# One masking instruction instead of two on GpSimd, routing's units spread over the attention stages, and a new order at the experts' entry

## The chip, the cores and the metric

The kernel runs on one core of a Trainium2 chip. The metric is the device time of one execution in microseconds (us); less is better. Engines are named as in the profile: PE (TensorE matmuls), PEld (TensorE weight loads), DVE (VectorE), ACT (ScalarE), POOL (GpSimd) and SP (SyncE, which issues most transfers).

## The reference

Attention with 4 sink keys and a causal window of 128 runs on 4 batches of 8 heads, 768 positions and a head dimension of 64. Its output, 3072 tokens of 512 numbers, goes through a mixture of experts: 4 groups of 4 experts, the best group and in it the best expert for each token, a hidden layer of 1024.

```python
scores = np.where(is_sink | in_window, scale * q @ k.T, -1e9)
a = np.exp(scores - scores.max(-1)); a = a / (a.sum(-1) + 1e-9)
x = (a @ v)                       # as [3072, 512]
g_idx = argmax(x @ w_group); g_w = softmax(x @ w_group)[g_idx]
e_idx = argmax(x @ w_expert[g_idx]); e_w = softmax(...)[e_idx]
out[token] = g_w * e_w * (relu(x @ w1[g, e]) @ w2[g, e])
```

## The kernel before

**Attention.** The first part is a loop over `i` from 0 to 25 (`NI` is 24). Each pass, called stage i here, works on three tiles of 128 tokens at once: the scores and exponentials of tile i, the transposes and the products with the values of tile a = i-1, and the normalisation of tile b = i-2. Stages with i below 24 are "live"; stages 24 and 25 only finish tiles. All engine queues run in program order, so the order of the calls in the loop is the order in each queue.

Each tile has two halves g of four heads. `scores` writes `ps` on PE. `maxima(i, g, between)` on DVE first runs a predicated copy on `ps` and then four fused subtract-and-reduce instructions (`sm`, CUSTOM in the trace); it calls `between` after the copy, after the second and after the fourth of these, so a stage has six places between maxima. `exps` runs on ACT. `trans` transposes on PE, `evac` copies to `pw` on ACT, and `halves(i, g)` on POOL multiplies the four diagonal blocks of `pw` once by each of two triangle masks `tri`: one product goes to blocks 8 to 11, the other stays in blocks 0 to 3. `values` is the product of `pw` with the values on PE. It needs both products. For the second half it runs in the next stage, behind that stage's first scores. `out_evac` (ACT), `natural` and `logits` (PE) follow; `norm` (DVE) writes `xt`, which SP stores to DRAM (`xd`). `norm_logits` (DVE) writes `lw`, and `add_heads` (POOL) sums it one stage later. The logits lie in the same PSUM tile as the scores of the first half.

**Routing.** When a batch of 6 tiles has its logits, a generator (`route_batch`) turns them into expert choices and positions. Each `yield` ends one unit of one to three small instructions. A label that it yields says where the next unit may run: `"pe"` only where the loop calls `routing(1, ("pe",))`, `"rd"` only where `("rd",)` is named, None anywhere. A stage has a quota (`UNITS`, or `REND`): units run singly in the six places between maxima and behind the second half's transposes (`unit(4)`, before `norm`), and what is left of the quota runs at the end of the stage in one go. Near the end a batch builds two one-hot arrays, `bf` and `af`, in two parts of three tiles each, and PE multiplies them into the table `tab`. Batch 0 starts in stage 8, batch 1 in stage 14, batch 2 in stage 20, batch 3 behind stage 25. Batch 1 also picks the first expert (`pick_id`, which makes `id0` known), batch 2 the second.

**Weights.** Weights come in chunks of 128 by 1024 numbers through `rw`. Each is split into a high part (`whi`, ACT) and the remainder (`wlo`, DVE), in live stages in two halves, one per stage. From stage 15 on, `prefetch` loads one chunk in odd stages and in stages 21 to 23, if the expert is known. A chunk's first half is split two stages after its load or later, when the loop's own clock says that it has landed.

**Entry.** In stages 24 and 25 the first expert's work (`ew`) is mixed in by `next(ew)`: two transposes of gathered tokens, then groups of layer 1 (12 matmuls each, which need the first four chunks). The last 128 rows of that expert are gathered by POOL when batch 2 has been added to `tab`, and PE transposes them behind the seventh group. After stage 25 the rest of the experts runs, bound by PE.

Of the kernel before, what the change touches and what calls it, by code (L numbers as in the profile page):

```python
# [16 lines left out]
ALU = mybir.AluOpType  # L17
# [5 lines left out]
P = 128  # L23
B, H, S, D = 4, 8, 768, 64
NT = S // P
NI = B * NT
# [5 lines left out]
NE = G * EG  # L32
# [22 lines left out]
DVELAG = 1.5  # L55
XLEAD = 9
PEGAP = 1.6
REND, TSTEP = 6, 16
UNITS = {7:4,8:7,9:6,10:6,11:6,12:6,13:6,14:6,15:6,16:6,17:6,18:6,19:6,20:6,21:6,22:6,23:6}
HC = 3  # L60
LATE = 6
PELAG = 2.0
# [72 lines left out]
def moe_attention(tc, kqT, vN, vS, nsw, wgx, w1, w2, out):  # L135
    nc = Pinned(tc)
    v = nc.vector
    with ExitStack() as top, ExitStack() as att:
# [15 lines left out]
        def const(shape, dt, name):  # L154
            return cp.tile(shape, dt, name=name)
# [97 lines left out]
        dq = gp.tile([P, D], F32, name="xg")  # L253
# [35 lines left out]
        tri = const([P, 2, D], F32, "tri")  # L289

        def other_masks():
            v.tensor_scalar(tri[:, 0], dq, 0.0, None, ALU.is_le)
            v.tensor_scalar(tri[:, 1], dq, 0.0, None, ALU.is_gt)
            v.tensor_copy(m4[:, 2, ::BW // NSK], m4[:, 0, ::BW // NSK])
            v.tensor_copy(msk[:, 1], msk[:, 2])
            v.tensor_tensor(snk[0:D], snk[0:D], isu[0:D], ALU.mult)
            v.tensor_tensor(mc[0:D, 1], mc[0:D, 1], snk[0:D], ALU.add)
# [58 lines left out]
        def route_batch(i0, nb, lt, wk, pt, tab, na, pick=None):  # L356
            def sm(shape, name, dt=F32):
                return wk.tile([P, MAXB] + shape, dt, name=name, bufs=1)[:, 0:nb]

            on = nc.gpsimd if pt is None and not tail else v  # L360
# [26 lines left out]
            oh = wk.tile([P, nb, NE], BF16, name=f"oh{nb}", bufs=1)  # L387
# [16 lines left out]
            pe = sm([NE], "pe")  # L404
# [42 lines left out]
            af = wk.tile([P, MAXB, NE, na], F32R, name=f"af{na}", bufs=1)  # L447
            bf = wk.tile([P, MAXB, P], F32R, name="bf", bufs=1)
            for j0 in range(0, nb, 3):
                j1 = min(nb, j0 + 3)  # L450
                w = j1 - j0
                v.tensor_tensor(bf[:, j0:j1], colm[:, None, :].to_broadcast([P, w, P]),
                                ga[:, j0:j1, None].to_broadcast([P, w, P]), ALU.is_equal)
                yield 2
                v.tensor_tensor(af[:, j0:j1], oh[:, j0:j1, :, None].to_broadcast([P, w, NE, na]),
                                av[:, j0:j1, None, :].to_broadcast([P, w, NE, na]), ALU.mult)
                if j1 < nb:
                    yield 2
            yield "pe"
            tt = misc(pt)[:, 0:NE * na]  # L460
            for j in range(nb):
# [204 lines left out]
        state = dict(issued=0, done=0, freed=0, credit=0.0, route=0.0, clk=0.0, at=0.0, dma=0.0, gap=PELAG, dve=0.0)  # L666
# [71 lines left out]
        def lg(i):  # L738
            o = 3 * BW + NSK
            if i < NI - 2:  # L740
                return psb[0][:, :, o:o + 2 * PW]
            if "lg" not in env[i]:
                env[i]["lg"] = spare()[:, 0:NDC * 2 * PW].rearrange("p (c n) -> p c n", c=NDC)
            return env[i]["lg"]
# [67 lines left out]
        def halves(i, g):  # L812
            pw = env[i]["pw", g]
            if i % NT:
                for k in (1, 0):
                    nc.gpsimd.tensor_tensor(pw[:, 8 * k:8 * k + 4], pw[:, 0:4],
                                            tri[:, k, None, :].to_broadcast([P, 4, D]), ALU.mult)

        def sink_copy(i):
            src = env[i]["pt"].rearrange("p m b l x -> p m (b l x)")[:, :, SW - NSK:SW + NSK]  # L820
# [27 lines left out]
        def values(i, g):  # L848
            pw = env[i]["pw", g]
            new, old = vts[i], vts.get(i - 1) if i % NT else None  # L850
            quarters(g, 0, P, new[:, 0], lambda d, j: pw[d, 2 * j:6 + 2 * j:5], start=g == 0)
            quarters(g, D, D, new[:, 1], lambda d, j: pw[d, 1 + 2 * j], stop=g == 1 and old is None)
            if old is not None:
                quarters(g, 0, P, old[:, 1], lambda d, j: pw[d, 4 + 2 * j:10 + 2 * j:5])
                quarters(g, 0, D, old[:, 0], lambda d, j: pw[d, 8 + 2 * j], stop=g == 1)
# [11 lines left out]
        def logits(i):  # L867
            for c in range(NDC):
                for f in range(2):
                    q = slice(f * D, (f + 1) * D)  # L870
                    nc.tensor.matmul(lg(i)[q, c], env[i]["xT"][:, c, q], wsd[:, c], start=True, stop=True)
# [39 lines left out]
                pick = {SNAP: 0, SNAPB: 1, len(BATCHES) - 1: 2}.get(k)  # L911
                rb.append([[(id(lt), x) for x in range(nb)], route(bounds[k], nb, lt, pick), None])

        def routing(k, kinds=(None, "pe", "rd")):
            while k > 0:
                if not rb or not have.issuperset(rb[0][0]):
                    return False
                kind = rb[0][2] if isinstance(rb[0][2], str) else None
                if kind not in kinds or (kind == "pe" and state["clk"] < state["at"]):
                    return False  # L920
                rb[0][2] = r = next(rb[0][1], "end")
                k -= r if isinstance(r, int) else 1
                if tail:
                    dve(0.6 if kind == "rd" else 0.25)
                state["at"] = max(state["clk"] + state["gap"], state["dve"] + 0.4)
                if rb[0][2] == "end":
                    rb.pop(0)
            return True
# [272 lines left out]
        quota = [0]  # L1201

        def unit(k):
            if quota[0] > 0 and routing(1, (None,)):
                quota[0] -= 1

        ew = early_work(PARTS[0][0])
        load_s(0)
        for i in range(NI + 2):
            live = i < NI  # L1210
            quota[0] = UNITS.get(i, REND)
            a, b = i - 1, i - 2
            mid, old = 0 <= a < NI, 0 <= b < NI
# [23 lines left out]
            if mid:  # L1237
                sink_copy(a)
                halves(a, 0)
            if not live:  # L1240
                next(ew)
                if not mid:
                    state["at"] = 0.0
                    routing(1, ("pe",))
            if mid:
                if not live:
                    next(ew)
                sink_t(a)
                trans(a, 1)
# [23 lines left out]
            if old:  # L1273
                natural(b)
            state["clk"] += 3.0
            if live and mid:
                values(a, 0)
            if old:
                logits(b)
            if i % 2 == 0 and 0 < i <= NI:  # L1280
                sums(i - 1)
            if not live:
# [13 lines left out]
            if live:  # L1296
                if mid:
                    halves(a, 1)
                exps(i, 1)
                trans(i, 0)  # L1300
                routing(1, ("rd",))
                unit(4)
                if old:
                    norm(b)
                if later and not gates:
                    gather(*later.pop(0))
                if late:
                    late()
                put_gates(2)
                routing(quota[0], (None, "rd"))  # L1310
            else:
                if mid:
                    next(ew)
                    values(a, 1)
                put_gates(MAXB)
                routing(TSTEP, (None, "rd"))
            if old:
                del env[b]
            if i >= CHOOK and (i % 2 or i > NI - 4):
# [299 lines left out]
```

## Time and profile before

| | us |
|---|---|
| median of three runs (lowest, highest) | 498.94 (498.5, 501.04) |
| profiled execution | 499.12 |
| its span, first to last instruction | 497.3 |
| PE, DVE, ACT, POOL busy in the span | 466.5, 347.0, 326.1, 170.3 |

The span leaves out 1.8 us around the program. Busy times are sums over the whole span; the attention part (about the first 157 us) and the expert part have different limits, so they are read apart.

### The profile page before, as it was taken

What the parts mean: (1) busy time and instruction counts of PE and PEld (TensorE: products, weight loads), DVE (VectorE), ACT (ScalarE), POOL (GpSimd) and SP (SyncE); (2) the same over time, 40 slices, a digit from 0 to 9 for tenths busy, and PEclk for the clock granted to TensorE, in tenths of its full rate; (3) what the DMA queues carried; (4) which work ended last, traced back from release to release, by engine and by line L of the source; (5) the groups of instructions that cost most, each with busy time, mean ns of one, the idle gap of its engine ahead of it and who ended that gap; (6) DMA issues with size and microseconds to landing.
All of it is one profiled execution on the core that took longest, in us unless ns stands there. A gap on an engine that the chain in (4) does not pass through costs nothing.

```text
span 497.3 us, 15548 instructions
## 1 busy us (share of the span) xinstructions
PE 466.5 (94%) x5865; PEld 396.2 (80%) x5865; DVE 347.0 (70%) x1147; ACT 326.1 (66%) x875; POOL 170.3 (34%) x303
## 2 busy tenths in 40 slices
PE   7999889988788998999999999999999999999995
PEld 6788778767667877889897967897879788877894
DVE  6677877897895777796137334844688888787870
ACT  4899779788774332575147247663878877687861
POOL 3565674583766002414020205120503071204021
PEclk9999999999998998999999999999999999999999
DMA  6566557476765529689215277986978997858200
GB/s 192 174 204 217 166 171 214 155 223 213 222 191 162 180 85 355 230 240 373 91 48 150 60 253 239 370 292 229 327 293 298 408 388 273 315 186 332 66 25 30
DMA packets 49556, 107.47 MB, mean 216 GB/s; under 512 B 8932, under 2 KB 9444, under 8 KB 49472
## 3 DMA queue, kind: packets, MB, share of 16 engines
q1 hardware_dynamic: 45008, 93.17, 56.0%
q0 software_dynamic: 4320, 12.94, 7.3%
q8 instruction: 48, 0.79, 0.7%
q10 hardware_dynamic: 144, 0.28, 0.2%
q14 instruction: 36, 0.29, 0.2%
HBM read 93.58 MB, written 12.93 MB: 214 GB/s over the span
## 4 chain that ended last, share of the span: by engine, by line
PE 65%; DVE 11%; ACT 9%; issue 8%; POOL 4%; DMA 2%; POOLq 0%; SPq 0%; DVEq 0%; ACTq 0%
PE po L105 29%; PE ph L105 29%; ACT pt L105 5%; PE tp L105 4%; PE ps L105 3%; POOL pw L105 2%; DVE wlo L105 2%; ACT pw L105 2%; DVE sm L105 1%; DVE xt L105 1%; ACT whi L105 1%; DMA qb<-in_kqT 1%; DVE ps L105 1%; POOL out L105 1%; DVE req L105 1%
## 5 line engine op out<-in xcount | busy, mean ns | idle before, releaser
L105 DVE TENSOR_TENSOR wlo<-rw,whi 128x1024 fp32r<-128x1024 f32 (+1 forms) x116 | 135.8, 1196 | 29.0 <-ACT whi L105 28.4
L105 PE MATMUL ph<-un,whi 128*128 128x256 f32 (+9 forms) x576 | 128.6, 313 | 0.0
L105 PE MATMUL po<-whi,un 128*128 128x512 f32 (+6 forms) x384 | 127.4, 397 | 0.0
L105 POOL DMA_INDIRECT out<-ot,sidx x33 | 41.0, 1244 | 225.4 <-ACT ot L105 169.6
L105 ACT CAST whi<-rw 128x1024 fp32r<-128x1024 f32 (+1 forms) x116 | 114.7, 1018 | 3.4 <-PE po L105 2.3
L105 PE MATMUL ph<-un,wlo 128*128 128x160 f32 (+10 forms) x416 | 99.5, 264 | 0.9 <-DVE wlo L105 0.9
L105 PEld LDWEIGHTS ph<-un,whi 128*128 128x128 f32 x576 | 93.8, 189 | 2.3 <-issue 1.0
L105 PEld LDWEIGHTS po<-whi,un 128*128 128x128 f32 (+5 forms) x384 | 70.6, 185 | 19.7 <-issue 2.1
L105 ACT ACTIVATE pt<-sm,st 128x136 f32<-128x136 f32 x192 | 76.3, 404 | 11.6 <-DVE st L105 11.4
L105 PE MATMUL po<-wlo,un 128*128 128x512 f32 (+7 forms) x200 | 78.7, 393 | 2.2 <-DVE wlo L105 2.2
L105 PEld LDWEIGHTS ph<-un,wlo 128*128 128x128 f32 x416 | 76.8, 189 | 1.5 <-DVE wlo L105 1.1
L105 POOL TENSOR_TENSOR pw<-pw,tri 128x256 f32<-128x256 f32 x80 | 60.1, 752 | 16.2 <-ACT pw L105 12.7
L105 DVE CUSTOM_DVE_ANT_0 sm<-ps,msk 128x136 f32<-128x136 f32 x192 | 46.9, 294 | 6.2 <-PE ps L105 1.1
L105 PE MATMUL po<-pw,vv 64*64 64x128 f32 (+1 forms) x1408 | 40.9, 252 | 9.9 <-POOL pw L105 6.2
L105 PEld LDWEIGHTS po<-pw,vv 64*64 64x64 f32 x1408 | 35.1, 135 | 17.8 <-POOL pw L105 8.5
L105 POOL DMA_INDIRECT xg<-xd,gidx x33 | 35.6, 1077 | 33.6 <-DVE idz L105 16.1
L105 PEld LDWEIGHTS po<-wlo,un 128*128 128x128 f32 (+6 forms) x200 | 36.0, 180 | 10.6 <-DVE wlo L105 2.6
L105 PE MATMUL ps<-kb,qb 64*64 64x204 f32 (+1 forms) x768 | 41.4, 330 | 2.7 <-DVE lw L105 2.2
L105 DVE TENSOR_TENSOR hc<-ph,hc 128x160 f32<-128x160 f32 (+6 forms) x64 | 21.4, 336 | 27.6 <-ACT hc L105 27.6
L105 ACT ACTIVATE un<-ph 128x256 fp32r<-128x256 f32 (+1 forms) x40 | 15.4, 384 | 35.7 <-PE ph L105 35.2
L105 ACT ACTIVATE ot<-po,cg 128x512 f32<-128x512 f32 (+7 forms) x25 | 17.0, 681 | 31.8 <-PE po L105 31.7
L105 ACT ACTIVATION_READ_ACCUMULATOR pt<-sm,st 128x1 f32 x192 | 37.2, 194 | 0.0
(200 smaller groups left out, 659.5 us busy)
## 6 DMA issues: line engine op xcount, KB each, us to landing
rw<-in_w SPq DMA_DIRECT2D x128, 512.0 KB, 5.5
kb<-in_kqT SPq DMA_DIRECT2D x23, 272.0 KB, 4.1
qb<-in_kqT SPq DMA_DIRECT2D x24, 256.0 KB, 3.5
vv<-in_vN SPq DMA_DIRECT2D x24, 256.0 KB, 3.5
xd<-xt SPq DMA_DIRECT2D x24, 256.0 KB, 2.4
xg<-xd,gidx POOLq DMA_INDIRECT x33, 5.9
out<-ot,sidx POOLq DMA_INDIRECT x33, 5.8
sv<-in_vS SPq DMA_DIRECT2D x4, 128.0 KB, 4.9
```

The lines of the kernel that those rows point to most:

```text
L105: r = f(*a, **k)
```

## The change

Six edits. `halves` issues one POOL instruction over both triangles, with the order of the masks in `tri` turned round. The quota is 8 in every stage, and the remainder no longer runs in one go: one unit more, `unit(5)`, runs at the end of the stage. `bf` and `af` get a label of their own, `"hv"`, one part for each live stage, at its end, and `af` goes to the engine called `on`, which is POOL for batches that start in a live stage. In live stages `logits(b)` comes ahead of `values(a, 0)`. In stage 25 the first `next(ew)` is gone. In stage 24 `values(a, 1)` comes ahead of a `next(ew)` instead of behind it.

```diff
-REND, TSTEP = 6, 16
-UNITS = {7:4,8:7,9:6,10:6,11:6,12:6,13:6,14:6,15:6,16:6,17:6,18:6,19:6,20:6,21:6,22:6,23:6}
+REND, TSTEP = 8, 16
+UNITS = {}
...
-            v.tensor_scalar(tri[:, 0], dq, 0.0, None, ALU.is_le)
-            v.tensor_scalar(tri[:, 1], dq, 0.0, None, ALU.is_gt)
+            v.tensor_scalar(tri[:, 1], dq, 0.0, None, ALU.is_le)
+            v.tensor_scalar(tri[:, 0], dq, 0.0, None, ALU.is_gt)
...
+                yield "hv"
                 v.tensor_tensor(bf[:, j0:j1], colm[:, None, :].to_broadcast([P, w, P]),
                                 ga[:, j0:j1, None].to_broadcast([P, w, P]), ALU.is_equal)
-                yield 2
-                v.tensor_tensor(af[:, j0:j1], oh[:, j0:j1, :, None].to_broadcast([P, w, NE, na]),
+                on.tensor_tensor(af[:, j0:j1], oh[:, j0:j1, :, None].to_broadcast([P, w, NE, na]),
                                 av[:, j0:j1, None, :].to_broadcast([P, w, NE, na]), ALU.mult)
-                if j1 < nb:
-                    yield 2
...
-                for k in (1, 0):
-                    nc.gpsimd.tensor_tensor(pw[:, 8 * k:8 * k + 4], pw[:, 0:4],
-                                            tri[:, k, None, :].to_broadcast([P, 4, D]), ALU.mult)
+                nc.gpsimd.tensor_tensor(pw.rearrange("p (k b) q -> p k b q", k=3)[:, ::-2],
+                                        pw[:, None, 0:4].to_broadcast([P, 2, 4, D]),
+                                        tri[:, :, None, :].to_broadcast([P, 2, 4, D]), ALU.mult)
...
-        def routing(k, kinds=(None, "pe", "rd")):
+        def routing(k, kinds=(None, "pe", "rd", "hv")):
...
-            if not live:
-                next(ew)
-                if not mid:
-                    state["at"] = 0.0
-                    routing(1, ("pe",))
+            if i == NI + 1:
+                state["at"] = 0.0
+                routing(1, ("pe",))
             if mid:
                 if not live:
+                    next(ew)
                     next(ew)
...
+            if old:
+                logits(b)
             if live and mid:
                 values(a, 0)
-            if old:
-                logits(b)
...
-                routing(quota[0], (None, "rd"))
+                unit(5)
+                routing(1, ("hv",))
             else:
                 if mid:
+                    values(a, 1)
                     next(ew)
-                    values(a, 1)
                 put_gates(MAXB)
-                routing(TSTEP, (None, "rd"))
+                routing(TSTEP, (None, "rd", "hv"))
```

## Rows read from the trace of the kernel before

**Rows 1.** Stretch; busy PE, PEld, DVE, ACT, POOL; PE's clock; DMA share, GB/s.

```profile
120.00:140.00 20.00, 16.18 (x420) 13.36 (x420) 17.04 (x76) 14.74 (x59) 12.20 (x21) 1.00 0.72 218
...
152.00:153.00 1.00, 1.00 (x18) 0.88 (x12) 0.00 (x0) 0.33 (x1) 0.92 (x2) 0.50 0.28 47
```

**Rows 2.** Timeline of SP's queue: start and length of stores of `xt`.

```profile
21.16 0.34 SPq L105 DMA_DIRECT2D xd<-xt  x1
...
47.34 0.34 SPq L105 DMA_DIRECT2D xd<-xt  x1
...
150.54 0.33 SPq L105 DMA_DIRECT2D xd<-xt  x1
```

**Rows 3.** Timeline of DVE: first unit of a stage's remainder, next predicated copy.

```profile
60.02 0.16 DVE L105 TENSOR_TENSOR runb<-runb,rs 128x16 bf16<-128x16 bf16 x1
...
60.93 0.42 DVE L105 COPY_PREDICATED ps<-selu,ps 128x256 f32<-128x256 int32 x1
...
128.53 0.28 DVE L105 TENSOR_TENSOR rdt<-lt,row 128x120 f32<-128x120 f32 x1
...
130.94 0.41 DVE L105 COPY_PREDICATED ps<-selu,ps 128x256 f32<-128x256 int32 x1
```

**Rows 4.** Timeline of DVE: maxima of stage 16 (six units) and 19 (none).

```profile
97.62 0.42 DVE L105 COPY_PREDICATED ps<-selu,ps 128x256 f32<-128x256 int32 x1
...
100.95 0.18 DVE L105 TENSOR_REDUCE rc<-sacc 128x16 f32<-128x32 f32 x1
...
117.28 0.42 DVE L105 COPY_PREDICATED ps<-selu,ps 128x256 f32<-128x256 int32 x1
...
120.24 0.32 DVE L105 TENSOR_TENSOR lw<-ps,rc 128x160 f32<-128x160 f32 x1
```

**Rows 5.** Instructions grouped by shape: count, busy us, mean ns, idle before.

```profile
L105 POOL TENSOR_TENSOR pw<-pw,tri 128x256 f32<-128x256 f32 x80 | 60.1, 752 | 16.2 <-ACT pw L105 12.7 <-DVE st L105 0.3
L105 POOL TENSOR_TENSOR lt<-lw 128x20 f32<-128x20 f32 x23 | 5.6, 242 | 1.8
L105 DVE TENSOR_TENSOR bf<-colm,row 128x384 fp32r<-128x384 f32 x6 | 3.6, 603 | 0.0
L105 DVE TENSOR_TENSOR af<-oh,av 128x336 fp32r<-128x336 bf16 x6 | 3.3, 550 | 0.0
L105 DVE SCALAR_TENSOR_TENSOR req<-rdt,row 128x120 f32<-128x120 f32 x4 | 2.7, 679 | 0.1
```

**Rows 6.** Timeline: the same `req` instruction with POOL busy and without.

```profile
128.84 1.04 DVE L105 SCALAR_TENSOR_TENSOR req<-rdt,row 128x120 f32<-128x120 f32 x1
129.01 1.53 POOL L105 TENSOR_TENSOR pw<-pw,tri 128x256 f32<-128x256 f32 x2
...
168.88 0.28 DVE L105 SCALAR_TENSOR_TENSOR req<-rdt,row 128x120 f32<-128x120 f32 x1
```

**Rows 7.** Waits up to 180 us: engine, releaser; total us, times, longest.

```profile
PE po L105 <- POOL pw L105: 6.2, 11, 2.1
...
DVE lw L105 <- POOL pw L105: 3.8, 6, 1.2
```

**Rows 8.** Timeline around the end of stage 23, all engines.

```profile
147.54 0.35 POOL L105 TENSOR_TENSOR cw<-rss 128x96 f32<-128x96 f32 x1 [1.11 <-DVE rss L105]
...
151.12 1.50 PE L105 MATMUL po<-pw,vv 64*64 64x128 f32 x32 [2.15 <-POOL pw L105]
```

**Rows 9.** Timeline of the first layer-1 group and the weight splits beside it.

```profile
157.23 0.28 PE L105 MATMUL ph<-un,wlo 128*128 128x256 f32 x1
157.24 0.71 DVE L105 TENSOR_TENSOR wlo<-rw,whi 128x512 fp32r<-128x512 f32 x1
...
161.99 1.23 DVE L105 TENSOR_TENSOR wlo<-rw,whi 128x1024 fp32r<-128x1024 f32 x1 [2.62 <-ACT whi L105]
```

**Rows 10.** Timeline: PE transposes the first expert's last gathered rows.

```profile
171.83 0.63 PE L105 MATMUL ph<-ident,xg 128*128 128x128 f32 x4 [1.23 <-DMA xg<-xd,gidx]
```

**Rows 11.** The chain that ended last: one layer-1 group of the first expert.

```profile
158.99 1.62 PE ph L105 x12
```

## Prediction
> **What bounds the kernel now.** I read the busy times by stretch first. Over the whole span PE is the busiest engine, and behind the entry it hardly waits. In the attention part that turns round: in 120 to 140 us DVE is busy for 17.0 of 20 us, PE for 16.2 [rows 1]. The reader is to see that no engine is full there; each waits for another in turn.
>
> The stores of `xt` give the pace. There is one each stage: from 21.16 to 47.34 us, before any routing, five stages take 26.2 us, 5.24 each. The next sixteen take 103.2 us up to 150.54 [rows 2]. At the old pace they would take 83.8, so 19.4 us are lost in stages 8 to 23, where routing and the first weight splits join in.
>
> Then DVE's own timeline. The remainder of a quota runs behind `norm` in one go, so the next predicated copy, and with it the maxima, starts later by all of it: 0.91 us in stage 9, 2.41 in stage 20 [rows 3]. A unit between maxima costs far less: with six of them stage 16 takes 3.33 us from its first copy to the end of its maxima, stage 19 without any 2.96 [rows 4], 0.06 each. The copy and the maxima leave gaps into which a small instruction fits.
>
> The table of waits shows the other coupling: PE waits for POOL's masked `pw` 11 times, 6.2 us in all, and DVE's `lw` 6 times, 3.8 us [rows 7]. The second is indirect: `lw` needs the logits, which stand in PE's queue behind the `values` that wait for `pw`.
>
> **The change part by part, against the profiled execution's 499.12 us.**
>
> *Routing's units.* Before, six stages (8, 9, 14, 15, 20, 21) run five units each in one go. I take the mean of the two shown, 1.66 us: 10.0 us. 24 small units lie between maxima, 1.5 us. Five pairs of `bf` and `af` lie there too, at 0.60 and 0.55 us [rows 5] 5.8 us. The sum, 17.3, accounts for most of the 19.4. After, I count 42 units between maxima by walking through the generator: 2.5 us. Ten stages get a `unit(5)` behind `norm`; at 0.30 each (a fifth of 1.66 is 0.33) 3.0 us. Five `bf` at stage ends are 3.0. `af` moves to POOL; by POOL's line below it takes 0.9 us there, behind `halves(a, 1)` and ahead of the next stage's first mask. DVE so sheds 17.3 - 8.5 = 8.8 us, from which the next item is taken.
>
> *The longer POOL instruction.* The `req` of stage 20 starts at 128.84 us and ends when POOL's first mask, begun at 129.01, is over: 1.04 us, against 0.28 with POOL quiet [rows 6]. The mean of the four is 0.68 [rows 5], so each loses 0.40 on average. POOL's line through 20 elements at 242 ns and 256 at 752 [rows 5] gives 512 elements 1.30 us, in place of 1.50 for two. The bounds are 1.30 (one fixed part saved) and 1.50 (none). A wait of 0.40 behind 0.75 grows to 0.69 behind 1.30. Of about 27 small units with two operands in SBUF I let one in three be hit: 9 by 0.29 is 2.6 us, between nothing (waits fall rarer, as POOL is held for less) and 7.8. The relief left is 6.2 us. A stage cannot go under 5.24, PE's pace, so I let two thirds reach the end: **-4.1**, with bounds 0 and -6.2.
>
> The Trainium skill, page "SBUF — State Buffer", section "Who interferes with whom", says that a DVE instruction with two SBUF inputs and a GpSimd one that reads SBUF exclude each other for the whole of an instruction. The pair shown agrees [rows 6]. By that rule alone merging lengthens every hold; the rows cannot say how many are hit, so it is a rival below.
>
> *The earlier end of the mask.* A pair takes 1.53 [rows 6], one instruction 1.30, so PE's 11 waits could shrink by 0.2 each, 2.5 at most. Most lie in stages that DVE paces: **-0.5**.
>
> *Logits ahead of `values(a, 0)`.* This takes `lw` out from behind `pw`: 3.8 us at most, but several of the six stages are paced by PE: **-0.8**. What could go wrong is that `logits` wait for the first half's maxima (same PSUM tile) with `values` now queued behind them; 0 is the other bound.
>
> *`cw` later on POOL.* `rss` becomes the last unit between maxima in stages 17 and 23 instead of the fourth. POOL's `cw` waits for it (1.11 us before [rows 8]), and behind `cw` on POOL are `add_heads` and `halves(a, 1)`, for which PE's next `values` wait: 2.15 us at 151.12 [rows 8]. About 2 us of instructions that stood behind `rss` now precede it, less `bf` and `af` (1.15), so PE waits some 1 us longer in stage 24. **+1.0**, between 0 and 2 (stage 18 as well).
>
> *Weights come two stages later.* This is not written in the diff. `id0` was known at the end of stage 15, in time for that stage's `prefetch`. Now stage 15 gets through only two of `pick_id`'s units, the rest follow in stage 16, and the next `prefetch` is in stage 17. One chunk fewer is split by stage 24: six `wlo` halves in place of eight. In stages 17 to 23 that takes two halves off DVE, **-1.2** (bounds 0 and -1.9). In stage 24 the fourth chunk must be split whole before the first layer-1 group can end. PE needed its low part at 157.23; DVE's half split ends at 157.95, and a whole one of 1.23 behind it at 159.18 [rows 9]: **+1.9**. On SP the next loads are then issued within that group, ahead of the loads that the end of the stage issued before.
>
> *Entry order.* In stage 25 `natural`, `logits`, `norm` and the table's last matmuls move ahead of one layer-1 group of 1.62 us [rows 11], and so do the store of `xt` on SP, the gather on POOL and batch 3's units. PE's wait of 1.23 us for that gather [rows 10] is shorter than the group: **-1.2**, or 0 if the earlier stall eats the lead. In stage 24 `values(a, 1)` and a group change places; both are issued anyway: 0. The group hides the evacuation of `xT` on ACT; without that cover it would be under 1 us.
>
> The sum: -4.1 - 0.5 - 0.8 + 1.0 - 1.2 + 1.9 - 1.2 = **-4.9**: 499.1 becomes 494.2. The median of the runs is 0.2 lower than the profiled execution, well inside the runs' own spread, so I give 494.2 for both.
>
> **The rivals.** *The lock takes it back* (no change). If every small two-operand unit meets a POOL mask (27 by 0.29 is 7.8 us), relief falls to 1.0 us, two thirds of it 0.7, and the sum to -1.5: 497.6. For it: `req` is hit in the mean of four. Against: POOL is held for less time in all.
>
> *The entry decides* (slower). The late first chunk costs 1.9 us, and `cw` up to 2.0. A PE that has stood still runs at half clock afterwards: the granted clock is 0.50 at 152 to 153 us, 1.2 instead of 2.4 GHz, after the wait of 2.15 [rows 1, 8]; that `values` block took 1.50 us. A second such stretch of 2 to 3 us at half speed costs 1 to 1.5. With the gather's gain lost this is +1.9 + 2.0 + 1.5, 5.4 us; it decides once the attention part gives back under 3 us, and with 2 us given back the time is 502.5. For it: all of it stands on PE's path. Against: the attention stages have 19.4 us of slack to give.
>
> *The spreading does not speed stages* (no change). If PE is the real limit in the routing stages, one third of the relief arrives, -2.1, and the sum is -2.9: 496.2, on the edge. Against: PE is idle for a fifth of 120 to 140 us [rows 1].
>
> **How the numbers follow.** The time forecast is 494.2, chance 0.50 with its neighbours from 491 to 496.4. The lock has 0.16, the spreading that brings little 0.14, the entry 0.20. About 0.5%, 2.5 us, is what a measurement tells from no change. Faster by more holds the forecast and a good third of the third rival: 0.55. Within it: 0.25. Slower: 0.20. The range starts from the sum with full relief (-6.2) and both POOL terms at their far ends (-2.5, -3.8 together in place of -1.3), 487 at the very least; these do not fall together, so I cut at 490. Above it takes in the lock and most of the entry case, 501.5. The forecast's own range is 491 to 496.4.
>
> **What would show it.** Right: 40 masks of 128x512 near 1.30 us; predicated copies closer behind `xt` in stages 9, 10, 15, 21 and 22; a pace under 6 us for stages 8 to 23 (6.45 before); `wlo` halves x6; no wait of PE for the last gather. Wrong: DVE units of over 1.2 us beside a mask (the lock); PE's wait in stage 24 well over 3 us, or a new stretch at half clock (the entry). If the masks take 1.5 us or more, the POOL terms fall. If stages 13 and 19, which now hold the wait for the table's matmuls, grow by over 1 us each, spreading has only moved the loss.

## The result and the profile after

The changed kernel takes 492.77 us (median of four runs, 491.73 to 493.08); the kernel before, beside it, 499.0 (498.5 to 501.04). The ratio is 0.9864 with a 95% interval of 0.9833 to 0.9895, so the change is faster by some 6.8 us of 500. The profiled execution took 493.08 us with a span of 490.8, against 499.12 and 497.3: 6.0 us less where the sum forecast 4.9. The number is close. What follows shows that its parts are not. (The spans differ by 6.5 us: 2.3 us of the execution now lie outside the span instead of 1.8. Every kernel below with the routing edits has 2.1 to 2.3 us there, every other 1.7 to 1.9; why was not looked into.)

Instructions grouped by shape up to 175 us (count, busy us, mean ns, idle before), to be held against [rows 5]:

```profile
L105 POOL TENSOR_TENSOR pw<-pw,tri 128x512 f32<-128x512 f32 x40 | 52.2, 1304 | 12.7 <-ACT pw L105 12.0 <-DVE st L105 0.3
...
L105 DVE TENSOR_TENSOR wlo<-rw,whi 128x512 fp32r<-128x512 f32 x6 | 5.2, 864 | 0.0
L105 POOL TENSOR_TENSOR af<-oh,av 128x336 fp32r<-128x336 bf16 x6 | 4.7, 786 | 0.0
...
L105 DVE SCALAR_TENSOR_TENSOR row<-ga,row 128x6 f32<-128x6 f32 x3 | 3.0, 991 | 0.0
...
L105 DVE SCALAR_TENSOR_TENSOR req<-rdt,row 128x120 f32<-128x120 f32 x4 | 1.1, 278 | 0.0
```

The merged mask takes the 1.30 us that the line through two sizes gave; `wlo` halves are six; `req` is at its quiet length of 0.28 instead of 0.68. Another unit has taken its place beside the masks: `row`, which the same view of the kernel before has at 0.16 us, takes 0.99 on average. On DVE's timeline one of the three lasts 1.26 us, over the 1.2 that I had named as a sign of the lock; POOL's mask runs beside it from 142.45 to 143.73.

```profile
L105 DVE SCALAR_TENSOR_TENSOR row<-ga,row 128x6 f32<-128x6 f32 x3 | 0.5, 160 | 0.0
```

```profile
142.49 1.26 DVE L105 SCALAR_TENSOR_TENSOR row<-ga,row 128x6 f32<-128x6 f32 x1
```

Stores of `xt` in the timeline of SP's queue, to be held against [rows 2]:

```profile
20.91 0.34 SPq L105 DMA_DIRECT2D xd<-xt  x1
...
48.46 0.34 SPq L105 DMA_DIRECT2D xd<-xt  x1
...
148.42 0.36 SPq L105 DMA_DIRECT2D xd<-xt  x1
```

From 48.46 to 148.42 there are sixteen stages of 6.25 us each, where they took 6.45 before and I had named under 6 as a sign of being right. Here is the first surprise: attention has hardly become faster. The maxima did move up, as DVE's timeline shows (stage 9, and stage 20, where the same `req` stands as in [rows 6]):

```profile
59.95 0.16 DVE L105 TENSOR_TENSOR runb<-runb,rs 128x16 bf16<-128x16 bf16 x1
60.03 0.41 DVE L105 COPY_PREDICATED ps<-selu,ps 128x256 f32<-128x256 int32 x1
...
127.53 0.28 DVE L105 TENSOR_TENSOR rdt<-lt,row 128x120 f32<-128x120 f32 x1
127.73 0.42 DVE L105 COPY_PREDICATED ps<-selu,ps 128x256 f32<-128x256 int32 x1
128.06 0.28 DVE L105 SCALAR_TENSOR_TENSOR req<-rdt,row 128x120 f32<-128x120 f32 x1
```

The copy follows 0.08 and 0.20 us behind the unit, where it came 0.91 and 2.41 later [rows 3]. But new waits stand elsewhere. The table of waits up to 175 us (total us, times, longest), against [rows 7]:

```profile
POOL cw L105 <- DVE rss L105: 5.4, 3, 2.4
...
PE po L105 <- POOL pw L105: 4.6, 2, 2.8
...
PE ps L105 <- DVE st L105: 3.8, 4, 1.6
DVE tab L105 <- PE tp L105: 3.5, 2, 1.7
```

`lw` no longer waits for `pw`, and of PE's eleven waits for `pw` two are left. Those two are long. They lie in stages 18 and 24, and POOL's timeline and PE's show what they hang on, against [rows 8]:

```profile
104.34 0.35 POOL L105 TENSOR_TENSOR cw<-rss 128x96 f32<-128x96 f32 x1 [2.43 <-DVE rss L105]
...
105.87 1.26 POOL L105 TENSOR_TENSOR pw<-pw,tri 128x512 f32<-128x512 f32 x1
...
107.18 1.13 PE L105 MATMUL po<-pw,vv 64*64 64x128 f32 x20 [1.75 <-POOL pw L105]
...
146.16 0.35 POOL L105 TENSOR_TENSOR cw<-rss 128x96 f32<-128x96 f32 x1 [2.43 <-DVE rss L105]
...
147.83 1.57 POOL L105 TENSOR_TENSOR pw<-pw,tri 128x512 f32<-128x512 f32 x1
...
149.45 0.79 PE L105 MATMUL po<-pw,vv 64*64 64x128 f32 x24 [2.82 <-POOL pw L105]
...
156.26 0.39 PE L105 MATMUL ph<-un,wlo 128*128 128x256 f32 x1 [1.53 <-DVE wlo L105]
```

Each time `cw`, issued in the stage before, holds POOL for `rss`, the second mask runs late behind it, and PE stands. The long `row` shown above stands ahead of `rss` on DVE, and DVE is not idle between them. The last row is PE's wait for the fourth chunk, split whole, to be held against [rows 9]. The wait for the last gather [rows 10] is gone. Stretches after the change (busy PE, PEld, DVE, ACT, POOL; PE's clock; DMA share, GB/s), against [rows 1]:

```profile
107.00:109.00 2.00, 1.82 (x44) 1.82 (x48) 0.00 (x0) 0.19 (x1) 2.00 (x4) 0.53 0.10 14
109.00:111.00 2.00, 2.00 (x42) 1.58 (x34) 1.14 (x10) 1.71 (x7) 1.08 (x4) 0.62 0.37 127
120.00:140.00 20.00, 15.90 (x420) 13.16 (x420) 18.16 (x90) 14.99 (x59) 13.75 (x19) 1.00 0.67 216
149.00:152.00 3.00, 2.55 (x58) 2.26 (x58) 0.41 (x1) 1.58 (x4) 2.55 (x4) 1.00 0.52 111
...
189.00:192.00 3.00, 3.00 (x16) 2.41 (x15) 2.87 (x11) 1.39 (x2) 0.42 (x1) 1.00 1.05 377
```

The wait in stage 18 is followed by four microseconds near 1.2 GHz, which cost 2 x 0.47 + 2 x 0.38 = 1.7 us. The kernel before has such a stretch too, in stage 24 [rows 1, 8], where the changed kernel has none; in attention the two cancel.

The second surprise lies behind attention. To see it I cut both traces at two events that have the same work ahead of them: the store of `xt` in stage 24, and PE's first product of layer 2.

| | before | after | difference | forecast |
|---|---|---|---|---|
| span's start to the store of stage 24 | 157.12 | 154.19 | -2.9 | -5.6 |
| from there to the first product of layer 2 | 22.64 | 23.49 | +0.85 | +0.7 |
| from there to the span's end | 317.54 | 313.12 | -4.4 | 0 |

(Forecast: -4.1 - 0.5 - 0.8 + 1.0 - 1.2 in the first row, +1.9 - 1.2 in the second.) Most of the gain comes from a stretch in which the prediction had no term. The kernel before shows there, on DVE, on PE and in its stretches:

```profile
185.33 0.17 DVE L105 SCALAR_TENSOR_TENSOR key<-cnt,col 128x16 f32<-128x16 f32 x1
...
186.75 1.22 DVE L105 TENSOR_TENSOR wlo<-rw,whi 128x1024 fp32r<-128x1024 f32 x1
```

```profile
188.02 0.50 PE L105 MATMUL po<-wlo,un 128*128 128x512 f32 x1 [2.15 <-DVE wlo L105]
```

```profile
189.00:192.00 3.00, 3.00 (x9) 2.35 (x8) 2.73 (x14) 2.00 (x3) 1.03 (x1) 0.50 1.05 388
```

The low part of layer 2's fourth chunk was split behind the first instructions of the experts' ranking (`key`, `big`, `rank`). PE waited 2.15 us for it, and the three microseconds from 189 went at half clock, 1.5 us more. After the change both splits come ahead of the ranking, and PE does not wait:

```profile
178.33 2.35 DVE L105 TENSOR_TENSOR wlo<-rw,whi 128x1024 fp32r<-128x1024 f32 x2
183.25 0.17 DVE L105 SCALAR_TENSOR_TENSOR key<-cnt,col 128x16 f32<-128x16 f32 x1
```

### The profile page after: what moved, and what is told of

Same layout as the page of the kernel before. It is cut to its first block, busy times and chain, and to the rows that moved or that the text cites. A ratio compares the mean times of both kernels' runs of the same rounds, so it can differ in the third digit from the quotient of the medians.

```text
span 490.8 us, 15503 instructions
## 1 busy us (share of the span) xinstructions
PE 464.5 (95%) x5865; PEld 395.1 (80%) x5865; DVE 340.6 (69%) x1140; ACT 325.6 (66%) x874; POOL 167.3 (34%) x269
## 4 chain that ended last, share of the span: by engine, by line
PE 70%; DVE 12%; issue 8%; ACT 6%; POOL 2%; DMA 1%; POOLq 0%; DVEq 0%
PE po L105 30%; PE ph L105 29%; PE ps L105 6%; PE tp L105 5%; ACT pt L105 3%; DVE wlo L105 3%; DVE sm L105 2%; DVE un L105 1%; DVE xt L105 1%; ACT whi L105 1%; POOL out L105 1%; DMA ni<-in_nsw 1%; ACT xT L105 1%; ACT pw L105 1%; DVE row L105 1%
## 5 line engine op out<-in xcount | busy, mean ns | idle before, releaser
L105 POOL DMA_INDIRECT out<-ot,sidx x33 | 42.3, 1282 | 220.4 <-ACT ot L105 163.8
L105 POOL TENSOR_TENSOR pw<-pw,tri 128x512 f32<-128x512 f32 x40 | 52.2, 1304 | 12.7 <-ACT pw L105 12.0
```

Source lines behind the costliest of these rows:

```text
L105: r = f(*a, **k)
```

## The experiments

Each is timed in five rounds against the kernel before. "Gain" is 500 us times one less the ratio. The two columns of trace times are the start of the first product of layer 2, and the time from there to the span's end. The profiled execution's distance from its own median says how far these trace times can be trusted: a microsecond or two.

| kernel | ratio, 95% interval | gain | profiled less median | first product | from there to the end |
|---|---|---|---|---|---|
| before | | | | 179.76 | 317.5 |
| after, all edits | 0.9864 [0.9833, 0.9895] | 6.8 | 0.3 | 177.68 | 313.1 |
| mask alone | 0.9939 [0.992, 0.9959] | 3.0 | -1.0 | 177.11 | 317.3 |
| routing alone | 0.9906 [0.987, 0.9941] | 4.7 | 2.1 | 181.20 | 314.1 |
| entry order alone | 0.9901 [0.9872, 0.9931] | 5.0 | -1.0 | 178.75 | 313.7 |
| logits alone | 1.002 [0.9988, 1.0052] | -1.0 | 1.9 | 182.75 | 319.2 |
| one split moved | 0.993 [0.9904, 0.9956] | 3.5 | -0.9 | 180.24 | 314.8 |
| after, less mask | 0.9864 [0.9828, 0.99] | 6.8 | 1.4 | 179.74 | 313.4 |
| after, less routing | 0.9938 [0.9915, 0.996] | 3.1 | 2.5 | 183.64 | 313.8 |
| after, less entry order | 0.9905 [0.987, 0.9939] | 4.8 | 0.8 | 179.33 | 314.3 |
| after, less logits | 0.9871 [0.9834, 0.9908] | 6.5 | -0.1 | 178.55 | 313.5 |
| after, `halves` earlier | 0.9915 [0.9889, 0.9942] | 4.3 | 0.4 | 181.22 | 313.1 |
| after, fourth chunk earlier | 0.987 [0.9839, 0.9901] | 6.5 | 0.4 | 178.45 | 313.8 |
| after, `cw` one unit later | 0.9836 [0.9808, 0.9864] | 8.2 | -1.5 | 174.31 | 313.6 |

The last column falls into two groups: 317.3 to 319.2 in the three kernels that have the wait at layer 2's fourth chunk, 313.1 to 314.8 in all others.

### The merged mask alone

```diff
-                for k in (1, 0):
-                    nc.gpsimd.tensor_tensor(pw[:, 8 * k:8 * k + 4], pw[:, 0:4],
-                                            tri[:, k, None, :]...)
+                nc.gpsimd.tensor_tensor(pw.rearrange("p (k b) q -> p k b q", k=3)[:, ::-2],
+                                        pw[:, None, 0:4]..., tri[:, :, None, :]...)
```

> The kernel before with one edit: one POOL instruction over both triangles. By the prediction's sum: 40 masks of 1.30 us, 0.5 us faster than before (0 to 2.5). If the longer hold on DVE decides (the lock rival): DVE's req and other units with two SBUF operands beside a mask take up to 1.3 us, their mean rises, and the time is 1 to 3 us longer than before.

Measured: 3.0 us faster, where the prediction's term was 0.5. In the table of waits up to 175 us and among the shapes it shows:

```profile
PE ps L105 <- DVE st L105: 3.2, 5, 1.3
PE po L105 <- POOL pw L105: 3.2, 6, 1.8
```

```profile
L105 DVE TENSOR_TENSOR req<-req,row 128x120 f32<-128x120 f32 x4 | 3.3, 819 | 0.1
...
L105 DVE SCALAR_TENSOR_TENSOR key<-oh,key 128x16 f32<-128x16 f32 x1 | 1.2, 1248 | 0.0
```

PE's waits for `pw` fall from 6.2 to 3.2 us [rows 7]. DVE's `lw` has no wait named after `pw` any more, but one of 4.9 us in all for PE's logits, which was 3.0; so 1.9 of its 6.8 us are gone. The lock is there too: one `key` of 16 columns takes 1.25 us beside a mask, and the second `req` 0.82 on average (0.42 in the kernel before). Six stages (8, 14, 17, 18, 20, 23) become 0.35 to 0.72 us shorter, stages 10 and 16 0.55 longer. The first product of layer 2 starts 2.65 us earlier, the rest is as before. So the mask's gain is in attention, six times what I gave it; the interval is 2.0 to 4.0 us, and the bound that I gave, 2.5, lies in it.

### Routing's units alone

```diff
-REND, TSTEP = 6, 16
+REND, TSTEP = 8, 16
+UNITS = {}
...
+                yield "hv"
                 v.tensor_tensor(bf[:, j0:j1], ...)
-                yield 2
-                v.tensor_tensor(af[:, j0:j1], ...)
+                on.tensor_tensor(af[:, j0:j1], ...)
...
-                routing(quota[0], (None, "rd"))
+                unit(5)
+                routing(1, ("hv",))
```

> The kernel before with the routing edits alone (quota 8, no remainder in one go, unit(5), the label hv, af on POOL). By the prediction's sum, -4.1 for the units, -1.2 for the two wlo halves, +1.9 for the fourth chunk and +1.0 for cw: 2.4 us faster. By the trace after, which shows PE waiting 1.75 us (and then 3.4 us at half clock) in stage 18 and 2.82 in stage 24 for the mask behind cw: the stages gain some 4 us and lose as much again, so within 1.5 us of before. With two masks in place of one these waits should be about 0.25 us longer each.

Measured: 4.7 us. By the last column 3.4 of that lie behind the first product, so little is left for the stages, for which the prediction had 4.1. Stages 8 to 11 together are 2.2 us shorter (23.61 from store to store, against 25.85); stages 13 and 19 are longer by 1.2 and 1.7. PE keeps eight waits for `pw`, 6.8 us in all, the longest 1.59 in stage 18 and 2.36 in stage 24. Both cases of the expectation were too low, since neither had the gain behind the first product.

### The entry order alone

```diff
-            if not live:
-                next(ew)
-                if not mid:
-                    state["at"] = 0.0
-                    routing(1, ("pe",))
+            if i == NI + 1:
+                state["at"] = 0.0
+                routing(1, ("pe",))
...
                 if mid:
-                    next(ew)
                     values(a, 1)
+                    next(ew)
```

> The kernel before with the order at the entry alone (stages 24 and 25). By the prediction's sum: 1.2 us faster (the wait for the last gather). By the trace after, in which DVE splits the first expert's last two chunks ahead of the ranking of the experts and PE no longer waits 2.15 us at the fourth w2 chunk, with 3 us at half clock behind it: 4 to 5 us faster, with no PE wait at that chunk.

Measured: 5.0 us. The trace has no wait for the gather and none at layer 2's fourth chunk: 1.0 us earlier at the first product, 3.9 us less behind it. The first is the term of the prediction (1.2); the second is not in it.

### One split moved, nothing else

In the kernel before, the split of 186.75 us is put ahead of the index selection. In the trace no other instruction of PE, DVE, ACT or POOL changes its place; on SP two weight loads move up.

```diff
         def final_pick(wk):
+            if tail:
+                wjob(True)
             yield from select(wk, 1, 0, NTR[1])
```

> The kernel before with one VectorE instruction moved and nothing else: the weight half that is split at 186.75, behind the ranking's key, big and rank, is split ahead of the index selection that comes before them (a 128x1024 subtraction of 1.22 us, some 2 us earlier in VectorE's queue); all other instructions of all engines keep their order, the attention stages too. Theory from the runs so far: both the spreading alone (4.7 us) and the entry order alone (5.0 us) got most of their gain here, by taking away TensorE's wait of 2.15 us at the fourth chunk of the second layer and the half clock of some 3 us behind it: then the wait named after wlo near 188 is gone, the granted clock of 189 to 192 is 1.00 instead of 0.50, and the time is 495 to 497.5 us, ratio 0.991 to 0.996. Rival: the wait hides slack of the experts, and without it the time is lost again at a later chunk or at the ranking that now comes 1.2 us later: 498 to 500 us, ratio 0.998 to 1.002, and the gains of those two runs have to be found in the stages.

Measured: 3.5 us, interval 2.2 to 4.8. The split on DVE, the next wait on PE, and the stretch:

```profile
184.88 1.22 DVE L105 TENSOR_TENSOR wlo<-rw,whi 128x1024 fp32r<-128x1024 f32 x1
```

```profile
202.46 0.38 PE L105 MATMUL ph<-un,wlo 128*128 128x248 f32 x1 [1.19 <-DVE wlo L105]
```

```profile
189.00:192.00 3.00, 3.00 (x14) 2.44 (x13) 2.73 (x14) 1.25 (x2) 1.19 (x2) 1.00 1.06 412
```

The wait of 2.15 us is gone, the stretch of half clock too; a later wait grows by 0.33 (1.19 against 0.86 before). 2.15 + 1.5 - 0.33 = 3.3 us, close to the run's 3.5; the trace has 2.8 less behind the first product. This settles that in the kernel before the order of two things on DVE, far behind the edits, is worth about half of what the whole change brings. Routing alone and the entry order alone both bring that order about (in both traces the splits stand ahead of `key`), so their single gains count it twice.

### The logits ahead of `values(a, 0)` alone

```diff
-            if live and mid:
-                values(a, 0)
             if old:
                 logits(b)
+            if live and mid:
+                values(a, 0)
```

> The kernel before with one edit alone: logits(b) ahead of values(a,0) on TensorE. Theory of the sum: the logits' matmuls end earlier, so the half row's maxima and the second half start earlier by about the length of one values group (0.8 us per two stages at most, -0.8 in all): about 498.5 to 499.5 us, ratio 0.995 to 0.999. Rival: in the kernel before VectorE's bursts of leftover work stand between the exponentials' copies and the maxima, so that TensorE gets to the logits before VectorE has made the half that they read; values(a,0), which was the work to fill that wait, now stands behind it. Then waits of 1 to 2 us named after VectorE's st appear ahead of the logits in the stages with bursts, as in the run without the spreading, and the time is 500 to 503 us, ratio 1.002 to 1.01.

Measured: 1.0 us slower, interval from 0.6 faster to 2.6 slower; no gain is shown. PE's logits now wait for the maxima eight times, 8.3 us in all, where the kernel before has four such waits of 2.6 in all. On PE's timeline:

```profile
135.35 0.67 PE L105 MATMUL ps<-wsd,xT 128*64 128x40 f32 x16 [1.83 <-DVE st L105]
...
145.00 0.67 PE L105 MATMUL ps<-wsd,xT 128*64 128x40 f32 x16 [2.02 <-DVE st L105]
```

That is what the prediction said could go wrong with this edit, with 0 as the bound; it came true while DVE's bursts hold the maxima up.

### The changed kernel with one edit taken back

Without the mask's merge:

> The changed kernel with the two separate mask instructions again (80 of 752 ns instead of 40 of 1304). Theory of the prediction's sum: the merge is worth the 0.2 us by which a half's masks end earlier, in few stages, 0.5 us in all: 493.3 us, ratio 0.987. Theory from the run of the mask alone (3.0 us by itself): the wait of TensorE for the masks in stage 24 grows from 2.82 to about 3.0 and those of 1 to 2 us in the even stages come back, 495 to 496 us, ratio 0.991 to 0.993. Rival, the lock: two short instructions hold VectorE's single rows for less time at once than one long one; then the time does not grow at all, 492 to 493 us, and VectorE's rows beside a mask are shorter than in the changed kernel.

Without the routing edits:

> The changed kernel with the routing of before (mask, logits and entry edits stay). By the prediction's sum the routing edits are worth 2.4 us (-4.1 - 1.2 + 1.9 + 1.0): 2.4 us slower than the changed kernel, ratio to before 0.991. If what they gain in the stages is lost again in stages 18 and 24 and at the first layer-1 group, and the wait at the fourth w2 chunk is gone by the entry order anyway: the same as the changed kernel within 1 us, or up to 2 us faster (ratio 0.982 to 0.988), since mask and entry alone already add up to 8 us.

Without the entry order:

> The changed kernel with the entry order of before. Alone, the entry order gave 1.0% (5 us), most of it PE's wait at the fourth w2 chunk with its half clock; but the routing edits alone had no such wait either. If the two share that gain: the changed kernel loses only the wait for the last gather, 1 to 2 us (ratio to before 0.988 to 0.991). If each brings its own: it loses 4 to 5 us (ratio 0.995 or more) and the wait at the fourth w2 chunk is back.

With `values(a, 0)` ahead of the logits again:

> The changed kernel with values(a,0) ahead of logits(b) again. Theory of the sum: it loses 0.8 us, 493.5 us. Rival: since the spread units leave VectorE free at that place, the wait for st (3.8 us over 4 waits in the first 175 us of the changed kernel) is all that the order costs now, and the values group would fill it: 489 to 492 us, ratio 0.977 to 0.985; the waits named after st go and those named after POOL's pw (2.82 in stage 24) stay.

Measured: the routing edits are worth 3.7 us here (0.9938 against 0.9864, intervals that do not overlap), the entry order 2.0, the logits 0.4 and the mask nothing; the intervals of the last three overlap with that of the whole.

The entry order answers to the first case of its expectation: the splits stay ahead of `key`, and PE stands 1.31 us before it transposes the last gathered rows. For the routing edits neither case was right, and for the logits the sum (0.8) was nearer than the rival. Without the routing edits PE's waits for the maxima add up to 10.7 us in nine, the longest 2.3, and the second `req` takes 0.91 us on average; I take this for bursts, lock and the new order of the logits together. Here all of the loss lies in attention (first product at 183.64; its profiled execution is 2.5 us above its median, so some 4 us are left of the 6), since the last column stays at 313.8.

So the routing edits pay in company with the logits' new place. What they are worth without it no pair of runs shows. The mask alone gains ahead of the first product and the entry order alone mostly behind it, 3.0 + 5.0 = 8.0 us together, which is more than the six edits' 6.8; a kernel with these two alone was not run, and by this estimate it would be level with the fastest here.

The mask's 3.0 us are gone in company, and in the two stages with long waits the rows say where. Without the merge the table of waits and the shapes up to 175 us have

```profile
POOL cw L105 <- DVE rss L105: 3.2, 2, 1.6
```

```profile
L105 DVE SCALAR_TENSOR_TENSOR row<-ga,row 128x6 f32<-128x6 f32 x3 | 1.3, 444 | 0.0
```

Beside two short masks `row` is held for 0.44 us on average, beside one long mask for 0.99; `rss` behind it comes later by the difference, POOL is free 0.27 us sooner, and `cw` waits 2.43 us instead of 1.6. What the merge gains at the mask's end it loses ahead of `cw`: PE's waits in stages 18 and 24 are 1.84 and 3.09 us without it, 1.75 and 2.82 with it. That is the case of the lock in the expectation. For the other stages this was not followed up.

### `cw` one unit later

In the changed kernel `rss` and `cw` were one unit, the last one between maxima. A `yield` between them, and one fewer behind, puts `cw` behind the second mask on POOL.

```diff
             v.reciprocal(ss, s5[:, :, 0:2])
+            yield
             cw = ...
...
                 put_gates(nb)
-            yield
             tabv ...
```

> The changed kernel with cw in the unit behind rss, so that in stages 17 and 23 it runs behind the second half's mask on POOL; all else, add_heads too, keeps its place. If cw's wait for rss is what holds the mask: PE's waits of 1.75 (stage 18) and 2.82 us (stage 24) go under 0.7, stage 18 runs at full clock, and the time falls by 3 to 5 us against the changed kernel, with no new DVE stalls as when the mask itself was moved. If DVE sets the pace there: under 1 us.

Measured: ratio 0.9836 [0.9808, 0.9864], 491.61 us, the fastest kernel here; against the change as it was made the point is 1.4 us better, with intervals that overlap. POOL and PE in the two stages:

```profile
102.71 1.32 POOL L105 TENSOR_TENSOR pw<-pw,tri 128x512 f32<-128x512 f32 x1
...
104.22 0.34 POOL L105 TENSOR_TENSOR cw<-rss 128x96 f32<-128x96 f32 x1 [0.18 <-DVE rss L105]
```

```profile
105.39 0.90 PE L105 MATMUL po<-pw,vv 64*64 64x128 f32 x32
...
146.10 0.90 PE L105 MATMUL po<-pw,vv 64*64 64x128 f32 x32 [0.70 <-POOL af L105]
```

The second mask starts at 102.71 instead of 105.87 and `cw` waits 0.18 us instead of 2.43. Stage 18 falls from 8.24 to 5.07 us, stage 24 from 5.77 to 3.65; stages 20 and 21 give back 1.0 and 1.1, and PE's granted clock is 0.57 over the four microseconds from 121 to 125, in stage 20, where the changed kernel has 1.00. At the first product 3.4 us remain in the trace, of which the execution's own distance from its median may explain half. So the waits went as expected, and the time fell by less than the 3 to 5 us expected.

### `halves(a, 1)` ahead of the second half's maxima

The other way to free the mask from `cw`: issue it before `maxima(i, 1)`.

```diff
-            if mid and not live:
+            if mid:
                 halves(a, 1)
...
-                if mid:
-                    halves(a, 1)
                 exps(i, 1)
```

> The changed kernel with the second half's mask issued on POOL ahead of the second half's maxima, so ahead of cw and add_heads. If cw's place in POOL's queue is what holds PE in stages 18 and 24: PE's waits of 1.75 and 2.82 us for pw go to under 0.5 each, the half clock in stage 18 goes too, and the time is 3 to 6 us below the changed kernel (487 to 490). If PE was held by DVE anyway in these stages: under 1.5 us better, or add_heads, now behind the mask, delays a batch's start and nothing is won.

Measured: 0.9915, some 2.5 us slower than the change, with intervals that just touch. PE's waits for `pw` are gone, as wanted (stage 18 takes 5.51 us, stage 24 3.32). But on DVE and POOL:

```profile
128.76 1.62 POOL L105 DMA_INDIRECT xg<-xd,gidx  x1 [0.96 <-DVE xt L105]
...
129.23 0.28 DVE L105 TENSOR_TENSOR rdt<-lt,row 128x120 f32<-128x120 f32 x1
...
129.75 2.24 DVE L105 SCALAR_TENSOR_TENSOR req<-rdt,row 128x120 f32<-128x120 f32 x1
...
130.57 1.27 POOL L105 TENSOR_TENSOR pw<-pw,tri 128x512 f32<-128x512 f32 x1
```

One `req`, 0.28 us long when it is left alone, takes 2.24 and ends just behind POOL's mask, which began 0.82 us after it; stage 21, in which these rows lie, grows from 6.77 to 9.44. Three more units (`rdt` twice, `rm`) take 1.2 to 1.3 us beside masks in this run. My theory that earlier masks only help fell here: this is the prediction's rival of the lock, brought about by placing masks beside the maxima. The Trainium skill, page "SBUF — State Buffer", section "Who interferes with whom", has a DVE instruction with two SBUF inputs and a GpSimd one that reads SBUF shut each other out for a whole instruction; for the mask the row agrees. The gather is not what held it before that: `rdt`, which reads two SBUF tiles as well, takes its usual 0.28 us beside the same gather. What kept `req` until the mask began stays open.

### The fourth chunk picked earlier

```diff
                 unit(5)
+                if i == 15:
+                    routing(3, (None,))
                 routing(1, ("hv",))
```

> The changed kernel with three more units at the end of stage 15, so that the first expert is known there and the first chunk's split begins in stage 17 as before. If the late first chunk costs what the prediction gave (+1.9 at the first layer-1 group, -1.2 in the stages): eight wlo halves again, no PE wait of 1.5 us at the first layer-1 group, and 0 to 1 us faster than the changed kernel. If the split halves in the stages cost DVE more than the wait: 1 us slower or more.

Measured: 0.987, the same as the change. PE's wait of 1.53 us is gone and `wlo` halves are eight again, but stage 16, which now runs the units in one go, is 2.0 us longer (7.96 against 5.98). The run moves more than the split: PE's wait for `pw` in stage 18 is gone as well (5.40 us against 8.24), and stages 17 and 19 to 21 are longer. So it does not price the late chunk alone.

## Why the prediction came out right, and where it did not

**The number.** -4.9 forecast, -6.0 in the profiled execution, -6.2 by the medians. The likeliest case and its bounds held. But two errors cancel: attention gave 2.7 us less than forecast, the experts 4.4 more. That the sum came out is in good part luck.

**Relief of DVE, -4.1 and -1.2.** Right as a mechanism, too large in what arrived. Copies follow at once, and stages 8 to 12 are 3.35 us shorter together. Then the signs that I had named for "only moved" fired: stage 13 takes 6.21 us instead of 4.98 and stage 19 6.67 instead of 4.98, 2.9 us lost again. DVE stands 1.74 us in each of them for PE's `tp` before it can add to `tab`, and `xt` is behind `tab` in its queue:

```profile
81.51 0.27 DVE L105 TENSOR_TENSOR tab<-tab,tp 128x112 f32<-128x112 f32 x1 [1.74 <-PE tp L105]
81.70 0.68 DVE L105 TENSOR_TENSOR xt<-po,rc 128x512 f32<-128x512 f32 x1
```

Both stages stay at 4.96 to 5.12 us in each run without the routing edits. I had put a third of the relief down as lost everywhere; the loss sits in these two stages.

Another loss lies where no routing runs: stages 5 and 6 take 11.95 us together, 10.57 before. Every kernel with the logits' edit has 11.40 to 11.95 there, and PE stands 0.27 to 0.82 us in the middle of stage 6 with no wait that the profile shows; the others have 10.38 to 10.57, but routing alone has 11.41 and a gap of 0.61. So the logits' edit is not all of the reason, and the cause stays open.

**`cw`, +1.0 with bounds of 0 and 2.** The right place and the right chain, but under-sized. In stage 24 the wait grew by 0.67 us, from 2.15 to 2.82. In stage 18, which I had only within the upper bound, a new one of 1.75 came, and with it 1.7 us at half clock. The entry rival had priced such a stretch, in the wrong stage. Moving `cw` alone gave stage 18 back 3.2 us and stage 24 2.1. By the ratios that run is only 1.4 us faster than the change, which is inside my bounds; it is the waits that I had too small, and I had left out the lock on `row` ahead of `rss`.

**The mask, -0.5.** The instruction's length was right (1.304). Its worth was not: alone it is 3.0 us. I had let 0.2 us in few stages count, since DVE paces them; but PE's waits of 6.2 us and `lw`'s of 3.8 [rows 7] both hung on the mask's end, and the run takes 3.0 off the first and 1.9 off what `lw` waits in all. In company it is worth nothing that can be measured, and in the two stages that I followed the longer hold on DVE takes the gain back.

**The logits, -0.8.** Not there: +1.0 alone, -0.4 in company, neither told apart from nothing. The bound of 0 was the better value. `lw`'s waits for `pw` and for the logits did go (6.8 us before, 0.2 after; the mask alone leaves 4.9), but PE's logits wait for the maxima instead, 3.8 us in company and 8.3 alone.

**The fourth chunk, +1.9, and the gather, -1.2.** Both right as waits: one of 1.53 us came, and the one of 1.23 went and is back (1.31) without the entry order. What the chunk's wait is worth in time is not shown; the run that removes it is no faster.

**Entry order, 0 for what stands behind.** This is the step that failed, together with the routing item, which brings the same order about. I asked of the moved layer-1 group only what it does to the gather, and never followed DVE's queue further, to see which weight split the experts' ranking stands in front of. The kernel before had the row in its trace, a wait of 2.15 us with three microseconds of half clock behind it, and I had written that behind the entry PE "hardly waits". One moved instruction shows it to be worth 3.5 us in the kernel before. Which of the loop's counters puts that split ahead in each kernel was not tried apart.

**The rivals.** *The lock* is real and did not go away: in the changed kernel the mean `req` fell to 0.28 us, but `row` rose from 0.16 to 0.99, and a `key` of 16 columns took 1.25 and an `oh` 0.95 beside a mask. It took back what the mask gives by itself, yet the change gained. *The entry* cost 1.5 + 0.7 us, against more given back; the half clock of stage 18 is set off by that of stage 24 before. *Spreading that brings little* comes closest to what attention did: 2.9 of 5.6.

## What to carry to other kernels

Follow a reordered step to the end of every in-order queue that it touches, not only to the wait that it is aimed at: here about half of the gain was a 1.22 us subtraction that came out ahead of another generator's instructions, 30 us downstream. List every PE wait of over a microsecond before predicting, with the half-clock stretch behind it, and ask of each whether the change moves its releaser. Gains of edits that were measured one at a time add up to more than the whole when two of them remove the same wait, so take each out of the whole as well.

## What the hardware showed that was not expected

The half clock did not follow from the length of PE's wait. After 1.75 us (stage 18) the granted clock was 0.53 over the next two microseconds; after 2.82 us (stage 24) it stayed at 1.00; before the change, waits of 2.15 us were followed by 0.50 in stage 24 and again at 188 us. The changed kernel without the entry order has the same wait in stage 24 as the changed kernel, 2.83 us, and then a mean clock of 0.66 over ten microseconds. PE's stretches, of the changed kernel first:

```profile
150.00:160.00 10.00, 8.45 (x153) 1.00 0.69 204
```

```profile
150.00:160.00 10.00, 10.00 (x110) 0.66 0.65 220
```

Executions of one kernel differ in it too: two of the kernel before took 498.83 and 505.09 us with mean granted clocks of 0.993 and 0.980, and 0.013 of 500 us is about what lies between them. A price for an idle PE should therefore have two values, with and without some 1.7 us for the clock, and a difference of two microseconds between single traces can be the clock alone.

In one row (`req`, 2.24 us) a small DVE instruction lasted through a mask on POOL that began 0.82 us after it. A gather on POOL does not hold DVE in these traces: `rdt` takes its 0.28 us beside the one of 128.76 us, and in the changed kernel a weight split takes its usual 0.68 us inside the one of 126.20 us.
